# A third room for v, and the first unit of attention handed out ahead of the rest

## The chip, the core and the metric

The kernel runs on one core of a Trainium2 chip. The metric is the device time of one execution in microseconds, the median of several runs. The engines of the core are TensorE (PE, with its weight loads PEld), VectorE (DVE), ScalarE (ACT), GpSimd (POOL) and SyncE (SP), which here issues most of the transfers. Each engine takes its own instructions in order and waits on semaphores for the others.

## What is computed

Linear attention with complex decay over 768 tokens, for 4 batches and 8 heads of 48 elements, and two feed-forward layers (384 to 2048 to 384) behind it on the 3072 tokens:

```python
mag = np.sqrt(a_re * a_re + a_im * a_im)
scale = np.minimum(mag, 0.999) / (mag + 1e-06)
a_re_n, a_im_n = (a_re * scale, a_im * scale)
...
for t in range(S):
    ar, ai = (a_re_n[:, :, t, :, None], a_im_n[:, :, t, :, None])
    new_re = ar * S_re - ai * S_im
    new_im = ar * S_im + ai * S_re
    kv = np.einsum('bhd,bhe->bhde', k[:, :, t], v[:, :, t])
    S_re, S_im = (new_re + kv, new_im)
    y[:, :, t] = np.einsum('bhd,bhde->bhe', q[:, :, t], S_re)
...
h = x @ w_in
g = np.maximum(h, 0.0) + np.log1p(np.exp(-np.abs(h)))
return (g @ w_out).astype(np.float32)
...
h = x @ w_in
g = np.where(h > 0.0, h, alpha * (np.exp(np.minimum(h, 0.0)) - 1.0))
return (g @ w_out).astype(np.float32)
...
x = np.ascontiguousarray(attn_out.transpose(0, 2, 1, 3)).reshape(B * S, H * D)
x = _moe_ref(x=x, **moe_kwargs)
return _moe2_ref(x=x, **moe2_kwargs)
```

The weights arrive as 64-bit floats.

## The kernel before

**Units.** The tokens are cut into 12 units of 256, three to a batch, and each unit into two chunks of 128. For a unit, VectorE forms the cumulative decays (`norm`, `prep`: the lines of it are recorded under L28, as they go through a helper), then in `qk` the decayed queries (`big<-W,qr`) and the decayed keys (`big<-W,tmp`, called KP below). The keys are needed in two forms. Transposed they come from TensorE (`flip`, L296) for the first seven units and from VectorE and memory for the others; with tokens on the partitions they go to memory (`kd`, L271) and come back as `KN` (`load_N`, L327).

**Chunks.** `chunks(u)` then has, for each of the two chunks: scores (L334, two groups of four heads on TensorE), the causal mask on VectorE (P), the outputs from P, v and the state (`outputs`, L358 and L361), and the state's update with KN and v (`update`, L395). Units 0 to 2 and 11 are brought into the layout of the products by TensorE (`relay`, L384); the others go to memory (`xd`) and come back as `xr` (L847). In both cases `split` makes the two parts xh (ScalarE, L404) and xl (VectorE, L405) that the products read.

**v.** `self.V` has two rooms for a chunk's v. `update` of chunk i loads chunk i + 2 into the room that chunk i has just used, so that load waits on TensorE until chunk i's outputs and update are through. SyncE issues it, in line with all its other loads.

**Products.** The first layer goes in steps: eight for a unit, each with two blocks of 128 of the hidden width. `a_s1` is the first product, `a_elem` the softplus (three passes on ScalarE, then L545 and L550 on VectorE), `a_s2` the second product; step n has the first product of n, the elementwise part of n - 1 and the second product of n - 2. All matmuls of the products are recorded at L525. `w_step` decodes one of 32 weight tiles of the layer from 64-bit form, with four instructions on VectorE (L449, L451, L452, L405).

**What sets the order.** One function lets the attention go on between the products. `decays()` is a generator that yields after each piece of a unit's VectorE work, for unit after unit; `stream()` takes a step of it, runs the actions that have fallen due (`DLY` steps after a store the reload, `CH0` steps after the keys' store the start of `chunks(u)`), and then one step of the chunks. `adv(ns)` takes steps until the VectorE work handed out, by a rough count, has reached a due time. Before the first product it is called for `W1` = 24,000 ns, then for `W0` = 2,000 ns at a time with one `w_step` each, up to `G0` = 12, until unit 0's input of the products is there. In the loop over the products it is called twice a step for `STEP` = 2,000 ns. A scheduler of the language then settles the order on each engine, by its own model of when each instruction can run.

Of the kernel before, what the change touches and what calls it, by code (L numbers as in the profile page):

```python
# [38 lines left out]
class Attn:  # L39
    def __init__(self, tc, ctx, flags, bank, net, q, k, v, a_re, a_im):  # L40
        self.tc, self.nc = tc, tc.nc
        self.q, self.k, self.v, self.a_re, self.a_im = q, k, v, a_re, a_im
        P = lambda n, b, **kw: ctx.enter_context(tc.tile_pool(name=n, bufs=b, **kw))
        self.raw = P("raw", 1)
        self.tmp = P("tmp", 3)
        self.wp = P("wp", 1)
        self.bigp = P("bigp", 2)
        self.c1 = P("c1", 1)
        self.ct = P("ct", 1)
        self.kn = P("kn", 2)  # L50
        self.pp = P("pp", 2)
        self.zp = P("zp", 1)
        self.dr = P("dr", 2, space=DRAM)
        self.bank, self.net = bank, net
        self.vec = Paced(self.nc.vector)
        nc = self.nc
        self.mask = self.c1.tile([128, 1, 128], F32, name="mask")
        nc.gpsimd.memset(self.mask, 1.0)
        nc.gpsimd.affine_select(
            out=self.mask, in_=self.mask, pattern=[[0, 1], [1, 128]],  # L60
            compare_op=ALU.is_ge, fill=0.0, base=0, channel_multiplier=-1)
        self.eye = self.c1.tile([128, 128], F32, name="eye")
        nc.gpsimd.memset(self.eye, 1.0)
        nc.gpsimd.affine_select(out=self.eye, in_=self.eye, pattern=[[1, 128]], compare_op=ALU.is_equal,
                                fill=0.0, base=0, channel_multiplier=-1)
        self.T = self.c1.tile([128, 1, 2, 64], F32, name="T")
        nc.gpsimd.memset(self.T[:, :, 0, :], 1.0)
        nc.gpsimd.memset(self.T[:, :, 1, :], 0.0)
        self.X = self.c1.tile([128, 2, 17, 4], F32, name="X")
        self.mh = flags[:, 92:93]  # L70
        nc.gpsimd.memset(self.mh, -0.5)
        self.ph = flags[:, 93:94]
        nc.gpsimd.memset(self.ph, 1.5)
        self.place = self.c1.tile([128, 96], F32, name="place")
        nc.gpsimd.memset(self.place, 0.0)
        for r in range(2):
            o = self.place[64 * r:64 * r + 64, 48 * r:48 * r + 48]
            nc.gpsimd.memset(o, 1.0)
            nc.gpsimd.affine_select(out=o, in_=o, pattern=[[1, 48]], compare_op=ALU.is_equal,
                                    fill=0.0, base=0, channel_multiplier=-1)  # L80
        self.V = []
        for i in range(2):
            t = self.c1.tile([128, 400], F32, name=f"V{i}")
            nc.gpsimd.memset(t[:, 384:400], 0.0)
            self.V.append(t)
        self.s0 = flags[:, 0:12]
        self.fin = flags[:, 12:28].rearrange("p (a b) -> p a b", a=4)
        self.st, self.nx = {}, None
# [21 lines left out]
    def load_v(self, i):  # L110
        b, t0 = i // 6, (i % 6) * 128
        self.nc.sync.dma_start(
            out=self.V[i % 2][:, 0:384].rearrange("t (h d) -> t h d", h=8),
            in_=self.v[b, :, t0:t0 + 128, :].rearrange("h t d -> t h d"))

    def tmpt(self):
# [227 lines left out]
    def outputs(self, u, c):  # L344
        nc = self.nc
        i = 2 * u + c
        QT = self.st["qT", u][:, :, c * 128:(c + 1) * 128]
        V = self.V[i % 2]
        Pt = [self.st.pop(("P", c, g)) for g in range(2)]
        if i % 6 == 0:  # L350
            self.Z = self.bank("Z")[0:96, 0:384].rearrange("p (h e) -> p h e", h=8)
            self.zs = None
        zs = self.zs
        Y = self.bank("sc").rearrange("p (h t) -> p h t", h=4)
        for h in range(8):
            pr, i4 = h % 2, h // 2
            o = Y[64 * pr:64 * pr + 64, i4, :]
            nc.tensor.matmul(out=o, lhsT=V[:, 48 * h:48 * h + 64], rhs=Pt[h // 4][:, h % 4, :],  # L358
                             start=(h < 2), stop=(zs is None and h > 5), skip_group_check=True)
            if zs is not None:  # L360
                nc.tensor.matmul(out=o[0:48], lhsT=zs[:, h, :], rhs=QT[:, h, :],  # L361
                                 start=False, stop=(h > 5), skip_group_check=True)
        self.Y = Y
# [24 lines left out]
    def update(self, u, c):  # L388

        i = 2 * u + c  # L390
        V = self.V[i % 2]
        if i % 6 != 5:
            KN = self.st.pop(("N", u, c))
            for h in range(8):
                self.nc.tensor.matmul(out=self.Z[:, h, :], lhsT=KN[:, h, :], rhs=V[:, 48 * h:48 * h + 48],  # L395
                                      start=(i % 6 == 0 and h == 0), stop=False, skip_group_check=True)
            self.zs = self.zp.tile([96, 8, 48], F32, name="zs", tag="zs")
            self.nc.scalar.activation(out=self.zs, in_=self.Z, func=AF.Copy)
        if i + 2 < 24:
            self.load_v(i + 2)  # L400
# [11 lines left out]

CH0 = 7
DLY = 2
W0 = 2000
W1 = 24000
STEP = 2000
G0 = 12
GA = 4
R0 = 3  # L420
R1 = 2
# [35 lines left out]
END = object()  # L457
# [306 lines left out]
def quick(tc, keep, q, k, v, a_re, a_im, w_in1, w_out1, w_in2, w_out2, out):  # L764
    nc = tc.nc
    with ExitStack() as ctx:
# [32 lines left out]
        def chunks(u):  # L799
# [56 lines left out]
            X[u] = hi, lo  # L856
            yield

        def decays():
            for _ in A.norm(0):  # L860
                yield
            for u in range(NU):
                n = 0
                for _ in A.prep(u):
                    n += 1
                    if n == 2 and u + 2 < NU:
                        A.load_a(u + 2)
                    yield
                yield from A.qk(u)
                if u + 1 < NU:  # L870
                    A.load_qk(u + 1)

        step, acts = 0, []
        ch = {"gen": None}

        def stored(n, u):
            if n != "n":
                acts.append((step + DLY, lambda: A.load_T(u, n)))
                return
            def load():  # L880
                A.load_N(u, 0)
                A.load_N(u, 1)
            acts.append((step + DLY, load))

            def go():
                ch["gen"] = itertools.chain(ch["gen"] or (), chunks(u))
            acts.append((step + CH0, go))

        A.stored = stored
# [1 line left out]
        def stream():  # L891
            nonlocal step, acts
            main = decays()
            busy = True
            while busy or acts or ch["gen"]:
                if busy:
                    busy = next(main, END) is not END
                step += 1
                now_, acts = [f for s, f in acts if s <= step], [x for x in acts if x[0] > step]
                for f in now_:  # L900
                    f()
                r = next(ch["gen"], END) if ch["gen"] else None
                if r is END:
                    ch["gen"] = r = None
                yield r

        st = stream()
# [2 lines left out]
        def adv(ns):  # L910

            nonlocal held, due
            due += ns
            while A.vec.ns < due:
                if held is not None and now < 8 * (held - 1):
                    due = A.vec.ns
                    return
                try:
                    held = next(st)
                except StopIteration:  # L920
                    due = A.vec.ns
                    return
# [5 lines left out]
        A.load_a(1)  # L928
        for net.top in range(LA):
            net.w_load(net.top)  # L930
        adv(W1)
        while 0 not in X:
            adv(W0)
            if net.g < G0:
                net.w_step()
        XR, X2 = {}, {}

        def x_load(b):
# [14 lines left out]
        for n in range(8 * NU + 2):  # L953
            u, p = n // 8, n % 8
            now = n
            if n < 8 * NU:
                while u not in X:
                    adv(1000)
                if n == 8 * NU - 8:
                    for _ in st:  # L960
                        pass
                    actx.close()
                    late = lambda name, bufs, side: ctx.enter_context(
                        tc.tile_pool(name=name, bufs=bufs, side=side, reuse_waits="tile"))
                    net.wp += [late("wts2", 12, "left"), late("wts3", 4, "left")]
                    xps = [late("xb0", 1, "left")]
                    net.w_load(32)
                    net.w_load(33)
                    net.top = 33
                    x_load(0)  # L970
                if n == 8 * NU - 3:
                    x_split(0)
                while net.g < min(32, 4 * n + GA):
                    net.w_step()
                if net.g == 32:
                    net.w_end()
# [86 lines left out]
```

## Time and profile before

| | |
|---|---|
| Median of three runs | 1195.05 us (1192.0 to 1198.69) |
| The profiled execution | 1191.51 us, of it 1189.8 us span |
| TensorE matmul, weight load | 1012.8 us (85%), 946.1 us (80%) |
| VectorE, ScalarE | 810.5 us (68%), 668.5 us (56%) |
| TensorE's mean clock | 0.957 of 2.4 GHz |

How to read it: the first product starts at 115.86 us, the last unit's first product at 742 us. From there TensorE is all but full, with the second layer's weights still decoded up to some 810 us. Between these two times attention and first layer share the engines. A unit's stretch below runs from its first product to that of the next unit; in it TensorE does that unit's products and, in between, attention of the next one. The granted clock of a stretch is a mean of the two levels, 1.2 and 2.4 GHz, in parts of the higher.

### The profile page before, as it was taken

How to read it: one execution, taken by the hardware profiler on the slowest of the kernel's cores; microseconds unless marked ns; L12 is line 12 of the kernel's file. 1: busy time of each engine (PE TensorE's matmuls, PEld its weight loads, DVE VectorE, ACT ScalarE, POOL GpSimd, SP SyncE). 2: the span in 40 equal slices, each digit the busy share in tenths (PEclk: the TensorE clock that was granted, in tenths of full speed). 3: DMA queues.
4: the chain of work that ended last, by engine and by line, in shares of the span. 5: the costliest groups of instructions: out<-in, count | busy, mean ns of one | idle time of the engine just before them, and what ended most of it. 6: DMA issues, size and time to landing. Idle time of an engine off the chain costs nothing.

```text
span 1189.8 us, 18268 instructions
## 1 busy us (share of the span) xinstructions
PE 1012.8 (85%) x7106; PEld 946.1 (80%) x7106; DVE 810.5 (68%) x1521; ACT 668.5 (56%) x1207; POOL 2.2 (0%) x19
## 2 busy tenths in 40 slices
PE   0027889798789989877988999999999999999997
PEld 0016789787689989877888889989999999999996
DVE  4997998596979979786879888894434333343332
ACT  5734866364648566444554568994545444454443
POOL 0000000000000000000000000000000000000000
PEclk9999989798889999887989999999999999999999
DMA  7335451534536263545363665550101000000000
GB/s 231 139 120 145 126 133 43 134 97 83 155 66 179 70 158 115 139 116 137 97 166 107 164 184 174 175 173 1 53 1 53 1 1 27 1 27 1 28 1 29
DMA packets 101823, 114.51 MB, mean 96 GB/s; under 512 B 49760, under 2 KB 78944, under 8 KB 101728
## 3 DMA queue, kind: packets, MB, share of 16 engines
q1 hardware_dynamic: 90272, 105.40, 31.5%
q10 hardware_dynamic: 11456, 7.87, 2.2%
q8 instruction: 57, 0.93, 0.3%
q14 instruction: 38, 0.31, 0.1%
HBM read 77.86 MB, written 35.39 MB: 95 GB/s over the span
## 4 chain that ended last, share of the span: by engine, by line
PE 52%; DMA 22%; DVE 14%; ACT 6%; issue 3%; SPq 1%; ACTq 0%; DVEq 0%
PE b L525 42%; DMA kd<-big 7%; DMA KN<-kd 7%; DVE big L28 4%; DVE tmp L28 4%; PE b L334 3%; PE b L395 3%; DMA wr<-in_moe_w_in_dram 3%; PE b L358 2%; DMA wr<-in_moe_w_out_dram 2%; DMA xr<-xd 2%; ACT w L446 1%; ACT w L445 1%; PE b L361 1%; DMA xd<-ye 1%
## 5 line engine op out<-in xcount | busy, mean ns | idle before, releaser
L525 PE MATMUL b<-xh,w 128*128 128x256 f32 (+1 forms) x1728 | 406.2, 328 | 31.9 <-ACT xh L404 24.2
L525 PEld LDWEIGHTS b<-xh,w 128*128 128x128 f32 x1728 | 295.0, 197 | 55.2 <-ACT xh L404 26.2
L525 PE MATMUL b<-xl,w 128*128 128x256 f32 (+1 forms) x864 | 277.8, 325 | 0.6 <-DVE xl L405 0.6
L525 PE MATMUL b<-gh,w 128*128 128x256 f32 x1152 | 215.0, 288 | 1.7 <-ACT gh L548 1.7
L525 PE MATMUL b<-w,gh 128*128 128x384 f32 x768 | 190.8, 335 | 0.0
L525 PEld LDWEIGHTS b<-gh,w 128*128 128x128 f32 x1152 | 179.0, 195 | 3.9 <-ACT gh L548 2.1
L525 PEld LDWEIGHTS b<-xl,w 128*128 128x128 f32 x864 | 167.5, 196 | 12.9 <-DVE xl L405 1.0
L584 DVE SCALAR_TENSOR_TENSOR t<-t,b 128x512 f32<-128x512 f32 x96 | 65.9, 687 | 149.8 <-ACT t L582 149.8
L525 PE MATMUL b<-gl,w 128*128 128x256 f32 x576 | 158.5, 292 | 3.0 <-DVE gl L550 3.0
L525 PEld LDWEIGHTS b<-w,gh 128*128 128x128 f32 x768 | 140.0, 188 | 7.8
L525 PE MATMUL b<-w,gl 128*128 128x384 f32 x384 | 123.7, 335 | 0.0
L581 ACT ACTIVATE t<-b 128x512 f32<-128x512 f32 x96 | 57.2, 596 | 111.6 <-PE b L525 109.2
L405 DVE TENSOR_TENSOR gl<-t,gh 128x512 fp32r<-128x512 f32 x96 | 66.4, 691 | 71.6 <-ACT gh L404 70.4
L525 PEld LDWEIGHTS b<-gl,w 128*128 128x128 f32 x576 | 108.5, 196 | 4.8 <-DVE gl L550 4.0
L404 ACT ACTIVATE gh<-t 128x512 fp32r<-128x512 f32 x96 | 60.6, 631 | 77.0 <-PE b L525 71.8
L541 ACT ACTIVATE t<-b 128x512 f32<-128x512 f32 x96 | 56.8, 591 | 58.0 <-PE b L525 43.8
L296 PE MATMUL b<-eye,big 128*96 128x128 f32 x112 | 17.0, 294 | 82.3 <-DVE big L28 82.1
L548 ACT ACTIVATE gh<-t 128x512 fp32r<-128x512 f32 x96 | 60.0, 626 | 48.1 <-DVE t L545 24.6
L296 PEld LDWEIGHTS b<-eye,big 128*96 128x96 f32 x112 | 13.2, 135 | 83.3 <-issue 81.6
L28 DVE TENSOR_TENSOR P<-b,mask 128x512 f32<-128x512 f32 x48 | 33.0, 688 | 66.8 <-PE b L334 66.8
L395 PE MATMUL b<-V,KN 128*96 128x48 f32 x320 | 40.5, 288 | 43.2 <-DMA KN<-kd 43.2
L395 PEld LDWEIGHTS b<-V,KN 128*96 128x96 f32 x320 | 38.6, 206 | 46.0 <-issue 38.1
(114 smaller groups left out, 1550.3 us busy)
## 6 DMA issues: line engine op xcount, KB each, us to landing
wr<-in_moe_w_in_dram SPq DMA_DIRECT2D x32, 384.0 KB
wr<-in_moe_w_out_dram SPq DMA_DIRECT2D x32, 384.0 KB
dq<-big SPq DMA_DIRECT2D x12, 768.0 KB
qT<-dq SPq DMA_DIRECT2D x36, 256.0 KB
kd<-big SPq DMA_DIRECT2D x12, 768.0 KB
KN<-kd SPq DMA_DIRECT2D x20, 384.0 KB
ar<-in_a_re_dram SPq DMA_DIRECT2D x12, 384.0 KB
ai<-in_a_im_dram SPq DMA_DIRECT2D x12, 384.0 KB
```

What stands on the lines that cost most here:

```text
L28: return f(*a, **kw)
L296: nc.tensor.transpose(out=ps[0:96, 128 * i:128 * i + 128], in_=W[:, 96 * (4 * g + i):96 * (4 * g + i) + 96], identity=self.eye)
L334: self.nc.tensor.matmul(out=sc[:, h, :], lhsT=KT[:, 4 * g + h, :], rhs=QT[:, 4 * g + h, :], start=(h == 0), stop=(h == 3), skip_group_chec ...
L358: nc.tensor.matmul(out=o, lhsT=V[:, 48 * h:48 * h + 64], rhs=Pt[h // 4][:, h % 4, :], start=(h < 2), stop=(zs is None and h > 5), skip_gro ...
L395: self.nc.tensor.matmul(out=self.Z[:, h, :], lhsT=KN[:, h, :], rhs=V[:, 48 * h:48 * h + 48], start=(i % 6 == 0 and h == 0), stop=False, sk ...
L404: nc.scalar.activation(out=hi, in_=x, func=AF.Copy)
L405: nc.vector.tensor_tensor(out=lo, in0=x, in1=hi.bitcast(F32), op=ALU.subtract)
L525: self.nc.tensor.matmul(out=out, lhsT=lhsT, rhs=rhs, skip_group_check=True, **kw)
L541: nc.scalar.activation(out=t, in_=h, func=AF.Abs)
L548: nc.scalar.activation(out=gh, in_=t, func=AF.Copy)
L581: nc.scalar.activation(out=t, in_=h, func=AF.Relu, scale=-1.0)
L584: nc.vector.scalar_tensor_tensor(out=t, in0=t, scalar=-1.0, in1=h, op0=ALU.add, op1=ALU.max)
```

## The change

`V` gets a third room, and the load of chunk i + 2 goes into the room that chunk i - 1 has used. The scratch for descriptors shrinks from 1024 to 256. Before the first product, `stream()` is stepped one step at a time, with a `w_step` at each step after the sixth, up to 22 of the layer's 32 weights instead of 12. `decays()` sets `alone` when unit 0's keys are done and yields once more; while `alone` is set, the stream does not go on with the next unit's decays, until unit 0's input is there. The same holds while a later unit's input is waited for and chunks are open. If chunks of two units are open, the stream takes two steps of them. `adv` takes at most four steps at a call.

```diff
-        for i in range(2):
+        for i in range(3):
             t = self.c1.tile([128, 400], F32, name=f"V{i}")
...
-            out=self.V[i % 2][:, 0:384].rearrange("t (h d) -> t h d", h=8),
+            out=self.V[i % 3][:, 0:384].rearrange("t (h d) -> t h d", h=8),
...
-W0 = 2000
-W1 = 24000
+S0 = 6
 STEP = 2000
-G0 = 12
+STEPS = 4
+G0 = 22
...
+        def chunked(u):
+            yield from chunks(u)
+            ch["n"] -= 1
+
...
                 yield from A.qk(u)
+                alone["on"] = u == 0
                 if u + 1 < NU:
                     A.load_qk(u + 1)
+                if u == 0:
+                    yield
...
-                ch["gen"] = itertools.chain(ch["gen"] or (), chunks(u))
+                ch["gen"] = itertools.chain(ch["gen"] or (), chunked(u))
+                ch["n"] += 1
...
-                if busy:
+                if busy and not alone["on"]:
                     busy = next(main, END) is not END
...
-                r = next(ch["gen"], END) if ch["gen"] else None
-                if r is END:
-                    ch["gen"] = r = None
+                r = None
+                for _ in range(2 if ch["n"] > 1 else 1):
+                    if ch["gen"] and r is None:
+                        r = next(ch["gen"], END)
+                        if r is END:
+                            ch["gen"] = r = None
                 yield r
...
-            while A.vec.ns < due:
+            for _ in range(STEPS):
+                if A.vec.ns >= due:
+                    break
...
-        adv(W1)
         while 0 not in X:
-            adv(W0)
-            if net.g < G0:
+            next(st)
+            if net.g < G0 and step > S0:
                 net.w_step()
+        alone["on"], due = False, A.vec.ns
...
                 while u not in X:
+                    alone["on"] = bool(ch["gen"])
                     adv(1000)
+                alone["on"] = False
...
-                while net.g < min(32, 4 * n + GA):
+                while net.g < min(32, max(4 * n + GA, G0 + 2 * n)):
                     net.w_step()
...
-    nc = _bacc.Bacc("TRN2", target_bir_lowering=False, num_devices=1, dynamic_dma_scratch_size=1024)
+    nc = _bacc.Bacc("TRN2", target_bir_lowering=False, num_devices=1, dynamic_dma_scratch_size=256)
```

What the scheduler makes of it is seen at three places. The first is VectorE before the first product, where unit 0's first xl is made from the relayed bank; X and T belong to unit 1's decays, f and w to the decoding of weights. Before:

```order
L28 TENSOR_TENSOR tmp<-X 128x256
L28 TENSOR_TENSOR P<-b_582,mask 128x512
L452 SCALAR_TENSOR_TENSOR f<-wr,f 128x384
L28 TENSOR_TENSOR X<-tmp 128x64 x2
L405 TENSOR_TENSOR w<-f,w 128x384
L405 TENSOR_TENSOR xl<-b_630,xh 128x3x128
```

and after:

```order
L28 TENSOR_TENSOR tmp<-X 128x256
L28 TENSOR_TENSOR P<-b_598,mask 128x512
L452 SCALAR_TENSOR_TENSOR f<-wr,f 128x384
L28 TENSOR_TENSOR X<-tmp 128x64 x2
L405 TENSOR_TENSOR w<-f,w 128x384
L405 TENSOR_TENSOR xl<-b_620,xh 128x3x128
```

The same rows stand there, the xl as row 161 of VectorE before and 160 after: nothing has moved at this place.

The second is TensorE at the first update of unit 2, chunk 4 (L395), among unit 1's products; gh and gl are the elementwise results of a step. Before:

```order
L525 MATMUL b3_1755<-gh_2215,w_1430 128x256 x2
L525 MATMUL b3_1755<-gl_2216,w_1430 128x256
L334 MATMUL b4_1601<-qT_1243,kT_1542 128x128 x4
L334 MATMUL b5_1619<-qT_1243,kT_1542 128x128 x4
L395 MATMUL b7_548<-V0_137,KN_1360 96x48 x8
L358 MATMUL b4_1732<-P_1661,V0_137 64x128
```

and after:

```order
L525 MATMUL b2_1584<-gh_1858,w_716 128x256 x2
L525 MATMUL b2_1584<-gl_1859,w_716 128x256
L525 MATMUL b3_1585<-gh_1858,w_716 128x256 x2
L334 MATMUL b4_1885<-qT_1665,kT_1826 128x128 x4
L334 MATMUL b5_1903<-qT_1665,kT_1826 128x128 x4
L525 MATMUL b3_1585<-gl_1859,w_716 128x256
L395 MATMUL b7_581<-V1_139,KN_1726 96x48 x6
L525 MATMUL b2_1584<-gh_1966,w_793 128x256 x2
```

Before, all products of unit 1 stand ahead of the update and none behind it; after, products of unit 1 stand on both sides of it.

The third is TensorE at the first product of unit 5 (from xh), where unit 4's second products end. Before:

```order
L525 MATMUL b3_3616<-gh_4031,w_1283 128x256 x2
L525 MATMUL b3_3616<-gl_4032,w_1283 128x256
L525 MATMUL b1_4070<-xh_4066,w_289 128x256 x2
L525 MATMUL b6_4150<-xh_4066,w_358 128x256 x2
L525 MATMUL b0_4221<-xh_4066,w_471 128x256 x2
L525 MATMUL b2_3615<-gh_4130,w_1410 128x256 x2
L525 MATMUL b3_3616<-gh_4130,w_1410 128x256 x2
```

and after:

```order
L525 MATMUL b3_3505<-gh_4030,w_1054 128x256 x2
L525 MATMUL b3_3505<-gl_4031,w_1054 128x256
L296 MATMUL b4_4100<-eye_122,big_3985 96x128 x4
L296 MATMUL b5_4106<-eye_122,big_3985 96x128 x4
L525 MATMUL b1_3961<-xh_3957,w_201 128x256 x2
L525 MATMUL b6_4040<-xh_3957,w_265 128x256 x2
L525 MATMUL b0_4141<-xh_3957,w_352 128x256 x2
L296 MATMUL b4_4115<-eye_122,big_3985 96x128 x4
```

The transposes of unit 6's keys (L296) stood 63 rows behind unit 5's first product before; now they stand ahead of and among unit 5's first products, and unit 4's last second product is through before them.

## Rows read from the trace of the kernel before

**Rows 1.** The page's part 1: busy us, share of the span, instructions of each engine.

```profile
PE 1012.8 (85%) x7106; PEld 946.1 (80%) x7106; DVE 810.5 (68%) x1521; ACT 668.5 (56%) x1207; POOL 2.2 (0%) x19
```

**Rows 2.** Stretches: length, busy us of PE, PEld, DVE, ACT, POOL, clock, DMA, GB/s.

```profile
115.86:182.17 66.31, 55.96 (x460) 52.05 (x461) 61.60 (x116) 48.84 (x95) 0.00 (x0) 0.92 0.46 129
182.17:244.79 62.62, 53.98 (x444) 51.17 (x444) 46.30 (x109) 30.02 (x50) 0.00 (x0) 0.86 0.31 83
244.79:308.54 63.75, 50.03 (x416) 48.70 (x417) 51.47 (x97) 35.41 (x56) 0.00 (x0) 0.89 0.42 101
308.54:360.50 51.96, 46.69 (x397) 45.17 (x398) 43.44 (x85) 30.44 (x51) 0.00 (x0) 0.90 0.43 110
360.50:410.08 49.58, 47.38 (x436) 46.33 (x435) 45.87 (x87) 35.29 (x56) 0.00 (x0) 1.00 0.44 124
410.08:458.80 48.72, 45.36 (x395) 43.86 (x396) 41.19 (x82) 31.26 (x52) 0.00 (x0) 0.96 0.47 128
458.80:523.30 64.50, 53.69 (x457) 52.24 (x456) 51.82 (x95) 33.12 (x59) 0.00 (x0) 0.90 0.51 135
742.00:1189.80 447.80, 439.95 (x2337) 400.48 (x2335) 196.47 (x326) 238.03 (x437) 0.00 (x0) 1.00 0.12 39
```

**Rows 3.** Waits of TensorE in the whole span: us in total, times, longest.

```profile
PE b L395 <- DMA KN<-kd: 43.2, 11, 7.3
PE b L525 <- ACT xh L404: 24.2, 9, 8.1
```

**Rows 4.** Waits of VectorE, the row on the scores.

```profile
DVE P L28 <- PE b L334: 66.8, 25, 11.5
```

**Rows 5.** Two of VectorE's groups by shape: busy us, mean ns, idle before.

```profile
L28 DVE TENSOR_TENSOR big<-W,tmp 128x1536 f32<-128x1536 f32 x12 | 21.0, 1752 | 0.2
...
L405 DVE TENSOR_TENSOR w<-f,w 128x384 fp32r<-128x384 f32 x64 | 34.9, 552 | 3.0 <-ACT w L404 2.6
```

**Rows 6.** Timeline, unit 2: KP on VectorE, its store and reload on SyncE.

```profile
210.99 1.76 DVE L28 TENSOR_TENSOR big<-W,tmp 128x1536 f32<-128x1536 f32 x1
...
212.77 0.34 SPq L271 DMA_DIRECT2D kd<-big  x1
...
220.59 0.38 SPq L327 DMA_DIRECT2D KN<-kd  x1
```

**Rows 7.** Timeline of TensorE: first update matmuls of units 2 to 9, idle before.

```profile
228.93 1.32 PE L395 MATMUL b<-V,KN 128*96 128x48 f32 x7 [7.29 <-DMA KN<-kd]
...
279.81 1.49 PE L395 MATMUL b<-V,KN 128*96 128x48 f32 x8 [5.61 <-DMA KN<-kd]
...
334.72 0.52 PE L395 MATMUL b<-V,KN 128*96 128x48 f32 x2 [4.74 <-DMA KN<-kd]
...
386.69 1.47 PE L395 MATMUL b<-V,KN 128*96 128x48 f32 x15 [1.36 <-DMA KN<-kd]
...
436.85 1.19 PE L395 MATMUL b<-V,KN 128*96 128x48 f32 x12 [3.36 <-DMA KN<-kd]
...
491.99 1.33 PE L395 MATMUL b<-V,KN 128*96 128x48 f32 x7 [4.49 <-DMA KN<-kd]
...
553.43 1.81 PE L395 MATMUL b<-V,KN 128*96 128x48 f32 x10 [5.79 <-DMA KN<-kd]
...
609.39 1.83 PE L395 MATMUL b<-V,KN 128*96 128x48 f32 x10 [3.61 <-DMA KN<-kd]
```

**Rows 8.** A stretch full of products, columns as in rows 2.

```profile
258.00:264.00 6.00, 6.00 (x53) 6.00 (x52) 6.00 (x8) 4.58 (x8) 0.00 (x0) 1.00 0.72 221
```

**Rows 9.** Timeline of TensorE: first products of units 3 and 10, idle before.

```profile
308.54 1.65 PE L525 MATMUL b<-xh,w 128*128 128x256 f32 x6 [8.11 <-ACT xh L404]
...
695.73 0.97 PE L525 MATMUL b<-xh,w 128*128 128x256 f32 x6 [1.78 <-ACT xh L404]
```

**Rows 10.** Waits of SyncE's queue ahead of the loads of v (L112).

```profile
SPq L112 <- PE b L361: 154.5, 15, 23.1
SPq L112 <- PE b L358: 42.4, 4, 19.1
```

More of the change, by code (lines that the diff above doesn't have):

```diff
@@ L347, in outputs @@
         QT = self.st["qT", u][:, :, c * 128:(c + 1) * 128]
-        V = self.V[i % 2]
+        V = self.V[i % 3]
         Pt = [self.st.pop(("P", c, g)) for g in range(2)]
@@ L390, in update @@
         i = 2 * u + c
-        V = self.V[i % 2]
+        V = self.V[i % 3]
         if i % 6 != 5:
@@ L869, in decays @@
                 yield from A.qk(u)
+                alone["on"] = u == 0
                 if u + 1 < NU:
                     A.load_qk(u + 1)
+                if u == 0:
+                    yield
         step, acts = 0, []
-        ch = {"gen": None}
+        alone = {"on": False}
+        ch = {"gen": None, "n": 0}
         def stored(n, u):
```

## The prediction

> **What bounds the kernel now.** I read first the page's busy shares: no engine is full, TensorE 85% and VectorE 68% [rows 1]. Then the span cut at the first product of each unit of 256 tokens [rows 2]: after 742 us TensorE is busy 439.95 of 447.80 us at full clock. That is the second layer, which the change leaves as it is, so nothing can be won there. Before it, the stretches of 49 to 66 us differ from one another: in the one from 182.17 TensorE is busy 53.98 of 62.62 us and VectorE 46.30, in the one from 360.50 it takes 49.58 us with 47.38 busy. So both engines wait, and not always. TensorE's waits are two [rows 3]: 43.2 us on KN, the keys that go through memory and come back, and 24.2 us on xh, the attention's result made ready for the products. VectorE waits 66.8 us for scores [rows 4], because TensorE takes its instructions in order and the scores of a unit's second chunk stand behind the matmuls that want KN. After long waits the granted clock is lower: 0.86, 0.89 and 0.90 in the three stretches from 182.17 to 360.50, 1.00 in the next [rows 2]. At half clock work takes twice as long, so a stretch loses (1 - clock) times its length: 8.8, 7.0 and 5.2 us there.
>
> **The work itself.** No product, matmul or decode step is added or removed; VectorE, ScalarE and TensorE do the same work. The third room costs one memory fill, on POOL, which has 2.2 us of work in all [rows 1]. The smaller scratch only makes space. So every term is one of order.
>
> **Startup.** The unit handed out alone should leave VectorE earlier. The order says it hardly does: the same pieces of unit 1 still stand between unit 0's on VectorE, and the first xl comes after 160 rows instead of 161. Counting each row with the mean of its shape as in [rows 5], less the 0.08 us by which neighbours overlap, KP of unit 0 (the keys, the last big product of a unit on VectorE) comes 2.7 us of work earlier, but the second xl, which ends the preparation, 1.3 us later. Between them stands the same round trip of KN. I take 0 for the first product; the bounds are 2.7 us either way. In the stretch that follows VectorE is busy 61.60 of 66.31 us [rows 2], so VectorE's order prices it: 61.0 us of work between the second xl of unit 0 and that of unit 1 become 58.5. That is a gain of 2.5; I take **-2**.
>
> **KN.** One round trip worked out, unit 2: KP starts at 210.99 and takes 1.76 us, its store is issued at 212.77, the reload at 220.59 [rows 6], and the first matmul with KN starts at 228.93 after 7.29 us of idle [rows 7]. So 18 us pass from KP to KN, whatever the order. What hides them is the work that stands between on TensorE. In a full stretch 53 matmuls of a product take 6.00 us [rows 8], 0.11 us each. In the order of before, between the product whose elementwise part stands last ahead of KP on VectorE and the matmuls on KN, there are 90 product matmuls, 16 transposes and 8 score matmuls: 10.0 + 4.2 + 2.1 = 16.2 us (a quarter of a microsecond each for the latter). In the new order there are 166 and 16: 22.6 us. KP stands 1.5 us of VectorE work behind that elementwise part before and 0.6 now. Cover rises from 14.8 to 22.0 us, and 7.2 of the 7.29 us go.
> The same count for units 1 to 10, before: 17.2, 14.8, 21.2, 13.0, 20.0, 20.4, 17.3, 14.1, 13.4, 14.9. After: 15.6, 22.0, 30.0, 32.3, 18.6, 11.7, 13.6, 17.0, 13.5, 18.1. Where it rises, the wait of [rows 7] goes, at most by the rise: 7.2 (unit 2), 5.6 (3), 4.7 (4), 2.9 (8), in sum 20.4. Where it falls, a wait grows by the fall: 1.6 (1), 1.4 (5), 8.7 (6), 3.7 (7), in sum 15.4. Net **-5**. Bounds: -20 if the falls are covered, +15 if the rises buy nothing because the wait only goes to the next thing on the same chain.
>
> **xh.** The first product of a unit needs xl. I compare the VectorE work from the last elementwise part of the unit before to xl with the TensorE work between the same two products. Before, units 3 to 11: 1.4, -5.2, -0.8, -5.8, -3.9, -1.3, 0.4, 0.0, -6.2 us of excess; the wait is 8.11 us at unit 3 and 1.78 at unit 10 [rows 9], so an excess of some -4 waits nothing. After: -2.2, -1.8, 2.3, 1.2, -6.4, -2.5, -3.4, 0.0, -8.0. Taking 4 plus the excess, below zero as nothing, the sum goes from 19.8 to 21.6: **+2**. The waits move from units 3, 8 and 9 to 4, 5 and 6, where the new order puts KP and the transposes of the next unit ahead of this unit's first products. Bounds: -8, if the trip of the output through memory alone decides (matmul work behind the last output rises in units 3, 7, 8 and 9), and +5.
>
> **Clock.** In the three stretches from 182.17 to 360.50 the waits on KN of units 2 to 4 and the long one on xh shrink; the 21 us lost to the clock should fall by two thirds, -14. In the two stretches from 360.50 to 458.80, now nearly without loss (0 and 1.9 us), the new waits fall: 10 us on KN and 10 on xh more. I give them the loss that the stretches with such waits have now, 4 and 4 us: +8. Net **-6**, bounds -14 and +4.
>
> **Rooms for v.** SyncE, which issues the loads in order, stands 154.5 and 42.4 us in 19 waits for v's room [rows 10]. No engine waits for v, though, and the load of xr behind it waits for the attention output anyway. Price 0; the other end is the rival on freed loads. In four units the new order puts the load of xr behind those that wait for VectorE's transposes; that is in the xh term, as xl stands late there on VectorE too.
>
> **Sum.** -2 - 5 + 2 - 6 = -11 us on the profiled 1191.51, which lies 3.5 under the median of the runs: 1195.05 - 11 = **1184**. A second count, on VectorE alone: the idle for the scores [rows 4] is cover against chain, and the cover between KP and the second chunk's scores rises by 8.3 us of work in unit 2 (27 instructions become 39), by 1.6 to 2.8 in units 1, 3, 4 and 7, and falls by up to 1.5 in others, 14 us in sum. Some 5 of that I take off for unit 2, where TensorE's own work ahead of those scores grows too. That leaves -9; the two counts agree.
>
> **Rivals.** *Freed loads.* If SyncE's waits for rooms hold back the output's reload, the whole 24.2 us on xh go, with the rest as above but for its +2: 1195 - 13 - 24 = 1158, or 1170 where half of them give way to another wait. For it: the 197 us of waits. Against it: xr is issued right after its data has landed in every unit I looked at. The Trainium skill (Perfetto Trace Analysis, Optimization Strategy) says that gaps that repeat on an engine can mean too few buffers; by that rule the third room is the gain and this case the likely one, while no row here shows an engine that waits for v. With the lower bounds of the other terms, it gets 0.13.
> *Waits change places.* KN and xh net -3, no clock won, startup 0: 1189 to 1200, no change. For it: the attention's chain is as long as before and each unit still needs it. 0.27.
> *The lead costs more than it brings.* The new order has VectorE 12.4 and 17.6 us of work further in the attention when it comes to the first elementwise parts of units 5 and 6. TensorE stands at the transposes of unit 6, ahead of unit 5's first products, until KP of unit 6 is there: 10 us on KN, 10 on xh, 8 of clock, 28 us. It is given back only if unit 6's stretch, now 64.50 us, falls by some 14 (VectorE's part of it falls from 50.9 to 36.7). If half of that fails to come and unit 1's and 2's stretches win 8 instead of 14, the sum is +4 to +8: 1199 to 1203. It decides when the two stretches from 360.50 to 458.80 grow by over 30 us. 0.15.
>
> **How the numbers follow.** The forecast has 0.45, and its own range is 1173 to 1189. Half a per cent, 6 us, is about what a measurement of this kernel can tell from no change. Faster by more: forecast and freed loads, 0.58. Within: 0.27. Slower: 0.15. The range leaves out the far end of the freed loads and of the lead: 1166 to 1201.
>
> **What would show it.** First product at 116 us, within 2. Waits on KN from 43 to some 38, gone in units 2 to 4 and longer at 6 and 7. Stretches: unit 1's and 2's 7 us shorter each, those of units 4 and 5 together some 18 longer, unit 6's 14 shorter, the rest even; the clock near 0.95 in the first and under 0.95 in unit 5's. After the last unit's first product, 447 us as now. It is wrong if the first product comes much earlier, if KN waits stay in units 2 and 3, or if the stretches of units 4 and 5 do not grow.

## The result and the profile after

The changed kernel takes **1164.78 us** (median of 4 runs) beside 1194.19 for the kernel before: a ratio of 0.975, interval 0.9716 to 0.9784, 29 us. The profiled run took 1162.61 us, span 1160.8. The forecast was 1184 and its range began at 1166: the direction was right, the gain was more than twice what was counted.

Part 1 of the page after; [rows 1] is its counterpart.

```profile
PE 1001.1 (86%) x7106; PEld 933.2 (80%) x7106; DVE 810.4 (70%) x1521; ACT 667.2 (57%) x1207; POOL 2.2 (0%) x20
```

With the same 7106 matmuls, TensorE is busy 11.7 us less, and its idle time falls by 17.3 (29.0 of span less 11.7). Not all of the 11.7 can be put down to the clock: 3.3 of them lie ahead of the first product, where the rows show no higher clock after. The first row is the kernel before, the second the changed one, columns as in [rows 2]:

```profile
0.00:115.86 115.86, 25.79 (x157) 21.36 (x157) 90.56 (x205) 61.08 (x132) 2.22 (x19) 1.00 0.53 158
0.00:117.54 117.54, 22.46 (x156) 17.74 (x156) 90.67 (x209) 60.83 (x135) 2.24 (x20) 0.92 0.56 166
```

In units 0 to 10 the busy time falls by 9.0 (547.0 to 538.0), in the second layer it grows by 0.7.

Three waits of TensorE in the kernel before, beside those of [rows 3]:

```profile
PE b L296 <- DVE big L28: 82.1, 2, 81.6
...
PE b L525 <- DVE t L545: 7.4, 8, 2.2
...
PE b L334 <- DMA kT<-dk: 0.6, 1, 0.6
```

Where it waits after the change, and VectorE's row on the scores ([rows 3] and [rows 4]; us, times, longest):

```profile
PE b L296 <- DVE big L28: 86.5, 4, 80.6
PE b L525 <- ACT xh L404: 25.3, 9, 7.6
PE b L395 <- DMA KN<-kd: 15.6, 5, 6.8
PE b L334 <- DMA kT<-dk: 6.3, 2, 6.1
...
DVE P L28 <- PE b L334: 32.3, 13, 7.5
```

KN went from 43.2 to 15.6 and not to 38, xh from 24.2 to 25.3 (+2 was forecast), the scores from 66.8 to 32.3, 34 us where the second count had 9. The waits on KN fall by 27.6 us and all idle time by 17.3 only: kT takes back 5.7, the transposes (L296) 4.4 and xh 1.1. The chain that ended last says the same: the share of transfers on it falls. Its first line before, then after:

```profile
PE 52%; DMA 22%; DVE 14%; ACT 6%; issue 3%; SPq 1%; ACTq 0%; DVEq 0%
```

```profile
PE 58%; DMA 16%; DVE 13%; ACT 8%; issue 4%; SPq 2%; ACTq 0%; DVEq 0%
```

The stretches after, cut as in [rows 2]: units 0 to 10, then the second layer.

```profile
117.54:181.35 63.81, 56.54 (x461) 51.58 (x461) 60.45 (x124) 45.39 (x88) 0.00 (x0) 0.94 0.42 118
181.35:239.04 57.69, 50.85 (x444) 47.68 (x445) 49.81 (x103) 34.01 (x56) 0.00 (x0) 0.97 0.33 90
239.04:291.71 52.67, 46.81 (x416) 45.07 (x416) 48.76 (x91) 34.59 (x56) 0.00 (x0) 1.00 0.46 121
291.71:344.24 52.53, 49.66 (x433) 47.78 (x433) 48.18 (x89) 34.70 (x57) 0.00 (x0) 0.97 0.44 118
344.24:404.74 60.50, 51.64 (x424) 49.06 (x424) 51.09 (x92) 34.50 (x55) 0.00 (x0) 0.89 0.46 129
404.74:461.94 57.20, 48.47 (x408) 47.21 (x408) 49.99 (x90) 34.04 (x56) 0.00 (x0) 0.92 0.49 139
461.94:505.90 43.96, 41.74 (x343) 40.67 (x344) 37.30 (x77) 24.31 (x41) 0.00 (x0) 0.87 0.48 123
505.90:567.45 61.55, 53.14 (x457) 51.78 (x456) 48.58 (x91) 33.14 (x56) 0.00 (x0) 0.94 0.45 122
567.45:613.87 46.42, 46.33 (x400) 44.87 (x401) 42.77 (x86) 27.12 (x47) 0.00 (x0) 0.96 0.51 147
613.87:667.24 53.37, 47.63 (x437) 46.15 (x435) 49.10 (x90) 30.25 (x50) 0.00 (x0) 1.00 0.51 150
667.24:712.64 45.40, 45.23 (x392) 42.12 (x393) 35.97 (x64) 35.28 (x82) 0.00 (x0) 0.96 0.63 195
712.64:1160.80 448.16, 440.64 (x2344) 401.47 (x2342) 197.69 (x327) 239.03 (x438) 0.00 (x0) 1.00 0.12 39
```

Units 7 and 8 of the kernel before, which [rows 2] leaves out:

```profile
523.30:586.06 62.76, 51.93 (x401) 49.80 (x401) 47.66 (x87) 29.91 (x48) 0.00 (x0) 0.86 0.45 111
586.06:643.21 57.15, 48.69 (x400) 46.42 (x400) 48.00 (x90) 29.33 (x51) 0.00 (x0) 0.94 0.52 144
```

After less before: start +1.7; units 0 to 10: -2.5, -4.9, -11.1, +0.6, +10.9, +8.5, -20.5, -1.2, -10.7, +0.9, -0.9; second layer +0.4; in sum -29.0. More than half of it is there at the first product of unit 3 (308.54 before, 291.71 after: -16.8), and -12.2 comes behind it. This cut is used below.

### The profile page after: what moved, and what is told of

Same layout as the page of the kernel before. It is cut to its first block, busy times and chain, and to the rows that moved or that the text cites. A ratio compares the mean times of both kernels' runs of the same rounds, so it can differ in the third digit from the quotient of the medians.

```text
span 1160.8 us, 18255 instructions
## 1 busy us (share of the span) xinstructions
PE 1001.1 (86%) x7106; PEld 933.2 (80%) x7106; DVE 810.4 (70%) x1521; ACT 667.2 (57%) x1207; POOL 2.2 (0%) x20
## 4 chain that ended last, share of the span: by engine, by line
PE 58%; DMA 16%; DVE 13%; ACT 8%; issue 4%; SPq 2%; ACTq 0%; DVEq 0%
PE b L525 49%; DMA kd<-big 4%; DMA KN<-kd 4%; DVE big L28 3%; PE b L334 3%; DVE tmp L28 3%; PE b L395 2%; PE b L358 2%; DMA wr<-in_moe_w_out_dram 1%; ACT w L446 1%; ACT w L445 1%; DMA wr<-in_moe_w_in_dram 1%; PE b L361 1%; DVE W L28 1%; DMA kT<-dk 1%
## 5 line engine op out<-in xcount | busy, mean ns | idle before, releaser
L525 PE MATMUL b<-xh,w 128*128 128x256 f32 (+1 forms) x1728 | 405.6, 328 | 32.3 <-ACT xh L404 25.3
L525 PE MATMUL b<-gl,w 128*128 128x256 f32 x576 | 156.0, 286 | 1.4 <-DVE gl L550 1.4
L405 DVE TENSOR_TENSOR gl<-t,gh 128x512 fp32r<-128x512 f32 x96 | 66.4, 692 | 72.0 <-ACT gh L404 70.9
L296 PE MATMUL b<-eye,big 128*96 128x128 f32 x112 | 19.3, 320 | 86.8 <-DVE big L28 86.5
L548 ACT ACTIVATE gh<-t 128x512 fp32r<-128x512 f32 x96 | 60.0, 627 | 55.5 <-PE b L525 37.2
L296 PEld LDWEIGHTS b<-eye,big 128*96 128x96 f32 x112 | 14.8, 147 | 88.5 <-issue 85.5
L525 PEld LDWEIGHTS b<-w,gl 128*128 128x128 f32 x384 | 71.7, 188 | 0.1
L550 DVE TENSOR_TENSOR gl<-t,gh 128x512 fp32r<-128x512 f32 x96 | 65.4, 685 | 8.1 <-ACT gh L548 7.0
L545 DVE SCALAR_TENSOR_TENSOR t<-b,t 128x512 f32<-128x512 f32 x96 | 65.5, 683 | 5.6 <-ACT t L543 5.4
```

The costliest lines, as they stand in the source:

```text
L296: nc.tensor.transpose(out=ps[0:96, 128 * i:128 * i + 128], in_=W[:, 96 * (4 * g + i):96 * (4 * g + i) + 96], identity=self.eye)
L405: nc.vector.tensor_tensor(out=lo, in0=x, in1=hi.bitcast(F32), op=ALU.subtract)
L525: self.nc.tensor.matmul(out=out, lhsT=lhsT, rhs=rhs, skip_group_check=True, **kw)
L545: nc.vector.scalar_tensor_tensor(out=t, in0=h, scalar=0.0, in1=t, op0=ALU.max, op1=ALU.add)
L548: nc.scalar.activation(out=gh, in_=t, func=AF.Copy)
L550: nc.vector.tensor_tensor(out=gl, in0=t, in1=gh.bitcast(F32), op=ALU.subtract)
```

## The experiments

**One part undone, one part alone.** Two rooms for v in the changed kernel leave TensorE's and VectorE's orders as they are.

```diff
-        for i in range(3):
+        for i in range(2):
...
-        V = self.V[i % 3]
+        V = self.V[i % 2]
```

> The changed kernel with two rooms for v, as before; the order of the instructions on TensorE and VectorE is the same as in the changed kernel, row for row but for buffer names. Theory of the order (the gain comes from what stands between what on TensorE and VectorE): 1163 to 1168 us, as the changed kernel, and SyncE's waits for v grow from 201 us back towards 219 without an engine waiting for v. Rival of the rooms (the gain comes from loads that no longer stand behind the wait for v's room): 1180 to 1194 us, and TensorE's waits on KN or xh grow by 10 us or more.

> The changed kernel with two rooms for v; TensorE's and VectorE's orders are the same as in the changed kernel. Room theory: 5 to 8 us above the changed kernel of this call, 1170, with the waits for KN 5 us longer (20 against 15), in the stretches of units 5 and 7. Rival (the room does nothing): within 3 us of it.

> The changed kernel once more, beside three others on one chip. If the third room is worth what the first comparison showed (1164.8 here, 1170.9 with two rooms), it comes in at 0.975 of the kernel before and 6 us below the version with two rooms beside it; if that difference was one of chips, the two agree within 3 us.

Measured: 1170.87 (0.9828, 0.9781 to 0.9875) and, on another chip, 1168.75 (0.9798, 0.9757 to 0.984) beside 1163.29 (0.975, 0.9699 to 0.98) of the changed kernel. Both lie between the two ranges of the first expectation: most of the gain needs no third room, but not all of it. Side by side on one chip the room is worth 5.5 us, and none of the four runs with two rooms is as fast as the slowest with three; across chips it is 6.1 us by the times and 9 by the ratios. I take some 6. The intervals of the ratios overlap at their ends. Next, the new start in the kernel before (the change's lines on S0, G0, the start's loop and `alone` for unit 0; two rooms, single steps, no hold-back later):

> The kernel before with the new start alone (unit 0 alone, decode at each step up to 22 weights); two rooms, no holding back for later units, no double steps of the chunks. By the count of cover ahead of KN, units 2, 4 and 6 gain 6.4, 3.7 and 1.8 us, units 3, 7, 8 and 10 lose 3.1, 1.6, 1.2 and 6.1. Theory of the order, with falls counted in full: KN waits as before, 1186 to 1194 us. The same with falls that are covered elsewhere: KN waits down by 10 us or more, 1176 to 1185 us. Rival of the rooms: 1190 to 1196 us.

Measured: 1193.5, 1.0018 (0.9987 to 1.0049). Then the changed kernel without one of its two hold-backs:

```diff
-                alone["on"] = u == 0
+                alone["on"] = False
```

> The changed kernel without the one line that lets unit 0 go alone. The order falls back to near that of before (72% of TensorE's and 79% of VectorE's rows of the first layer match before, 47% match the changed kernel) although 22 weights are still handed out early, there are three rooms and the chunks go ahead. Theory of the order: 1188 to 1196 us, KN waits over 35 us. Rival of the rooms: 1165 to 1175 us. Rival of the weights (22 decoded early make the gain): 1165 to 1175 us.

```diff
-                    alone["on"] = bool(ch["gen"])
```

> The changed kernel without the line that holds the next unit's decays back while a later unit's input is waited for. The order is that of the new start alone, not of the changed kernel, from unit 2 on. Theory of the order: as the new start alone, within 3 us of it, and slower than the changed kernel by 8 to 25 us, with KN waits at units 3 and 4 that the changed kernel does not have. Rival of the rooms: 1163 to 1170 us, as the changed kernel.

Measured: 1191.78 (0.9991, 0.9964 to 1.0019) and 1192.71 (1.0013, 0.9977 to 1.0049). And the later hold-back alone in the kernel before; and the changed kernel with single steps (`range(1)` for `range(2 if ch["n"] > 1 else 1)`):

> The kernel before with the hold-back alone (chunks ahead of the next products), with the old start, two rooms, single steps. The start alone made no difference and the changed kernel without the hold-back none either. If the two only win together, this is within 4 us of the kernel before, 1187 to 1195. If the hold-back with single steps wins by itself, it is at 1165 to 1180.

> The changed kernel without the double steps where two units' chunks are at hand; its order differs from row 2455 of TensorE on, about from unit 7. If the gain is made by the start and the hold-back in units 1 to 6 (and by unit 6's stretch, which follows from them), this stays within 4 us of the changed kernel, 1161 to 1169. If the double steps make the gain of units 6 to 8 (some 30 us of it), it comes to 1175 to 1190.

Measured: 1201.44 (1.0069, 1.0035 to 1.0102), outside both theories: the later hold-back alone loses; and 1160.35 (0.9746, 0.9686 to 0.9806), so the double steps are worth nothing that shows. **In these runs the two hold-backs win only together.** The cap of four steps in `adv`, which the two single edits leave out, was not run apart. The steps of `stream()`, counted while the program is built, show how the two meet: before, 44 steps of the preparation are out at the first product, after 23. With the new start alone the product loop, waiting for unit 1, draws 19 more, and from unit 1's first product on the count is that of before to within one. With the later hold-back alone there is a lead of preparation, so the loop waits only at units 3, 5, 7 and 9, and the preparation is held for 30 steps in all. With both, it is held for 81: 15, 12, 14, 12, 12, 8, 0 and 8 steps at units 1 to 8. That these counts make the time is not shown.

In the three kernels that gain nothing, the waits on KN are down too, to 34 to 37 us. But without the later hold-back TensorE's busy time is up by 13 us, and its waits on an elementwise part of the products (t, L545) go from 7.4 to 15.4. Part 1 of that kernel's page, and its row on t:

```profile
PE 1026.0 (86%) x7106; PEld 955.9 (80%) x7106; DVE 812.1 (68%) x1521; ACT 668.3 (56%) x1207; POOL 2.2 (0%) x20
...
PE b L525 <- DVE t L545: 15.4, 13, 2.6
```

**The round trip itself.** The keys are reloaded from the store of the unit before, so that nothing waits for this unit's store.

```diff
-        kd = self.st["kd", u][:, c * 128:(c + 1) * 128, :]...
+        kd = self.st["kd", max(u - 1, 0)][:, c * 128:(c + 1) * 128, :]...
```

> The kernel before, with the keys KN of a unit read from the stored keys of the unit before it (the right keys are left out of the state's update; all loads, stores and matmuls stay). The reload no longer waits for this unit's store. The schedule moves some instructions for it. Theory 1 (the round trip of KN is what TensorE pays for, and the clock falls after it): the 43 us of waits on KN go to under 5 and the time comes down to 1145 to 1170, as far as the change or further. Rival (another wait takes its place, xh or the scores' kT on the same chain): KN waits gone, but the waits on xh and kT grow by 15 or more, and the time is 1180 to 1195.

> The same edit in the changed kernel. Theory 1: only the 15 us on KN that are left can go, 1145 to 1160, so that the difference between the two kernels with old keys is 10 us or less where it is 30 with the right ones. Rival: the changed kernel gains as little as the kernel before, and the 30 us between them stay.

Measured: 1177.18 (0.9863, 0.9779 to 0.9947) and 1160.31 (0.9714, 0.9641 to 0.9787). Neither theory hit the first, which lies between the two: 38 us of waits on KN go, 19 us of time (16 by the ratio). TensorE's waits in the kernel before with old keys:

```profile
PE b L334 <- DMA kT<-dk: 20.7, 5, 7.9
PE b L525 <- ACT xh L404: 16.5, 6, 5.9
...
PE b L395 <- DMA KN<-kd: 5.6, 1, 5.6
```

The second reload, kT, takes half of it over (0.6 before). The changed kernel had little left to gain there, 3 to 4 us; the two stay 17 us apart, where theory 1 had 10 or less and its rival 30.

**What stands in the trip.** Between the store of the keys and their reload SyncE issues ar and ai in units 0 to 8. A trip is here the time from the issue of that store to the first matmul with KN. (The trips of 14.9 to 21.4 us that are named below are those of units 2 to 8; units 0 and 1 took 14.0 and 11.5.) Without these loads from unit 2 on:

```diff
     def load_a(self, u):
+        if u >= 2:
+            self.st["a", u] = self.akeep[u % 2]
+            return
```

> The kernel before without the loads of ar and ai from unit 2 on (units use the data of units 0 and 1; the work on them stays). In the trace these two loads of 384 KB stand between the store of the keys and their reload in units 0 to 8, where the trip from the store's issue to the first matmul takes 14.9 to 21.4 us; in units 9 to 11, without them, 11.5 to 14.5. Collision theory: the trips of units 2 to 8 fall to 11 to 15, the waits on KN from 43 to 20 to 28, the time by 10 to 25. Rival (the trip has its length from the store and the reload themselves): trips within 1.5 us of the old ones, time within 6 us.

> The same edit in the changed kernel, where KN waits are 15 us and the two loads stand in the trip in units 0 to 7 only. Collision theory: 4 to 10 us faster, KN waits under 10. Rival: within 3 us.

Measured: 1162.11 (0.9744, 0.9673 to 0.9814) and 1136.26 (0.9506, 0.9436 to 0.9576): 34 us (31 by the ratio), and 29 by the ratios in the changed kernel, more than the collision theory had. The work left out is traffic only, so this is a price, not a version. The same loads moved, with nothing left out (from unit 3 on; in the third run they go behind the first KN of a unit, in the other two behind the last):

```diff
+            if behind is not None:
+                nc.gpsimd.tensor_copy(out=t[0:1, 0:1], in_=behind[0:1, 0, 0:1])
             nc.sync.dma_start(out=t, in_=s[b, :, t0:t0 + 256, :]...
...
-                    if n == 2 and u + 2 < NU:
-                        A.load_a(u + 2)
+                    if n == 2 and u == 0:
+                        A.load_a(2)
...
                 A.load_N(u, 1)
+                if u + 3 < NU:
+                    A.load_a(u + 3, A.st.get(("N", u, 1), A.st["N", u, 0]))
```

> The kernel before with the two loads of a (ar, ai, 384 KB each) issued behind the reload of the keys: an element of KN is copied on POOL into the first element of each room, so that the load waits until KN has landed; nothing is left out. Collision theory (the loads lengthen the trip of KN when they stand in it): trips of units 2 to 8 of 11 to 15 us, KN waits 43 to under 25, 1165 to 1182. Rival (the traffic costs as much wherever it stands): the waits move to kT, xh or to the store of the next keys, 1185 to 1200.

> The same edit in the changed kernel, behind the second KN. Collision theory: 1140 to 1156, KN waits under 8. Rival: 1158 to 1170, the change's own time.

> The changed kernel with the loads of a behind the first KN, which leaves its order nearer to that of the changed kernel (360 rows of difference on VectorE against 1160). Collision theory: 1142 to 1158. Rival: 1158 to 1170.

Measured: 1166.83 (0.9765, 0.9736 to 0.9794), 1152.76 (0.965, 0.9619 to 0.9681) and **1148.11** (0.9606, 0.9576 to 0.9637). All three lie in the ranges of the collision theory, and the last beats both kernels. The moved loads give back some 27 of the 34 us and some 16 of the 29; what the rest is was not looked into, and the schedule moves some instructions for the edit. The trip of unit 8 shows it: issues on SyncE (start, length) and the first matmul with KN, in the kernel before, then with the loads behind:

```profile
532.01 0.38 SPq L271 DMA_DIRECT2D kd<-big  x1
535.01 0.34 SPq L309 DMA_DIRECT2D dk<-big  x1
535.84 0.62 SPq L96 DMA_DIRECT2D ar<-in_a_re_dram  x1
536.66 0.60 SPq L96 DMA_DIRECT2D ai<-in_a_im_dram  x1
541.71 0.37 SPq L327 DMA_DIRECT2D KN<-kd  x1
...
553.43 1.33 PE L395 MATMUL b<-V,KN 128*96 128x48 f32 x7 [5.79 <-DMA KN<-kd]
```

```profile
518.58 0.42 SPq L273 DMA_DIRECT2D kd<-big  x1
521.58 0.34 SPq L311 DMA_DIRECT2D dk<-big  x1
528.38 0.37 SPq L329 DMA_DIRECT2D KN<-kd  x1
...
532.05 1.30 PE L397 MATMUL b<-V,KN 128*96 128x48 f32 x9 [1.95 <-DMA KN<-kd]
```

The store takes as long as before (9.7 and 9.8 us to the reload's issue); it is the reload, up to the first matmul, that falls from 11.7 to 3.7 us. In units 2 to 8 it took 6.6 to 11.7 before and takes 3.5 to 4.7 with the loads behind. The Trainium skill (DMA: Bandwidth & Descriptors, Rules for kernel authors) advises to issue a transfer early and to wait for it late; here loads issued as early as their room allowed cost 27 us in the kernel before and some 16 in the changed one, because they stood ahead of a reload that was waited for. The same section says that transfers issued from different engines all run on the same 16 DMA engines and interleave; no run here shows how they interleave, as SyncE issues all of these, and the trips show only that the reload takes 11.7 us with the two loads ahead of it and 3.7 without.

All kernels at the cut (first product of unit 3; from there to the end of the span), against the kernel before:

| kernel | to unit 3 | behind it | waits on KN |
|---|---|---|---|
| before | 308.54 | 881.3 | 43.2 |
| changed; again; single steps | -16.8; -15.1; -16.6 | -12.2; -14.8; -15.3 | 15.6; 14.7; 18.4 |
| changed, two rooms; again | -13.9; -15.1 | -7.0; -8.6 | 20.4; 17.6 |
| new start alone | -3.5 | +10.0 | 37.2 |
| without unit 0's hold-back | -3.9 | +2.3 | 34.2 |
| without the later hold-back | -7.5 | +13.6 | 34.5 |
| later hold-back alone | +8.8 | +5.2 | 45.9 |

And the changed kernel against the kernel before where both have the same edit:

| edit in both | to unit 3 | behind it | KN, before and changed |
|---|---|---|---|
| none | -16.8 | -12.2 | 43.2, 15.6 |
| old keys | -17.4 | -0.6 | 5.6, 5.2 |
| no loads of a | -21.8 | +1.9 | 9.6, 4.4 |
| loads of a behind the first KN (changed), behind the last (before) | -19.1 | -1.7 | 12.0, 2.7 |
| loads of a behind the last KN in both | -17.0 | +3.0 | 12.0, 5.2 |

These are single profiles, and the edits shift the order by themselves; but the four pairs with an edit say one thing. The gain up to unit 3 stays (3 to 4 us of it are the start's with old keys and with the loads behind); the 12 us behind it are there only while TensorE waits long for KN. With old keys neither kernel waits for KN behind the first product, and the gain up to unit 3 is still 17.4.

## Why the prediction was right and wrong

- **Up to unit 3: right in the numbers.** Forecast 0 for the first product, -2 for unit 0, -14 for units 1 and 2, in sum -16; measured +1.7, -2.5 and -16.0, in sum -16.8. The start came at 117.54, within the 2 us given. The waits on KN of units 1 to 3 fell by 10.1 where 11.2 were counted. But the pair with old keys keeps its gain there without any wait on KN, so that KN's cover makes it is not shown. The lead's price agrees in the sum too, +18 forecast for units 4 and 5 and +19.4 measured, but in part by luck, as the three parts it was made of add up to 28: the waits on xh in these stretches grew by 9.1 (10 counted) and the busy time by 7.4 (8 for the clock), while KN, counted at +10, fell by 2.1, and the transposes of unit 6 waited 4.8 for VectorE instead. In the whole span xh is +1.1 (+2 forecast).
- **The term that failed is KN from unit 3 on.** By the count the waits of units 3 to 10 change by -5.6, -4.7, +1.4, +8.7, +3.7, -2.9, 0, 0: +0.6. They changed by -5.6, -4.7, +0.1, -2.3, -2.3, -5.8, -3.6, -1.0: -25.1. (Units 0 to 2 gave 2.5 where 5.6 were counted: 3.95 us are left in unit 2, and the wait of unit 0, which was not counted, grew by 2.0.) In the whole span -27.6 stands where -5 was forecast, beyond the bound of -20; 10.3 us of it came back in TensorE's other waits. Two steps of the term were wrong.
- **First step: a fall of cover was made a wait of its own.** Only work was counted as cover. In units 6 and 7, where cover falls by 8.7 and 3.7, TensorE stands on something else during the same trip: +12.4 us were counted, -4.5 came. The changed kernel, idle before each in brackets; the keys are stored at 400.95 and at 453.30:

```profile
400.57 1.92 PE L296 MATMUL b<-eye,big 128*96 128x128 f32 x8 [4.82 <-DVE big L28]
...
404.74 1.65 PE L525 MATMUL b<-xh,w 128*128 128x256 f32 x6 [2.25 <-ACT xh L404]
...
417.29 0.88 PE L395 MATMUL b<-V,KN 128*96 128x48 f32 x8 [1.11 <-DMA KN<-kd]
...
461.94 1.65 PE L525 MATMUL b<-xh,w 128*128 128x256 f32 x6 [7.62 <-ACT xh L404]
...
472.63 1.68 PE L395 MATMUL b<-V,KN 128*96 128x48 f32 x12 [2.21 <-DMA KN<-kd]
```

  The waits on xh, 2.25 and 7.62 us, lie inside the trips, and products at a clock of 0.92 and 0.87 take longer: both hide KN. I had summed KN, xh and clock as if they followed one another. The bound "-20 if the falls are covered" named this; the value was taken too near the other end.
- **Second step: "18 us pass from KP to KN, whatever the order".** From the store's issue to the first matmul it is 11.5 to 21.4 us before. In unit 8 the new order issues the reload ahead of ar and ai, and the trip falls from 21.4 to 12.4. In unit 9 it falls from 14.5 to 11.4; neither load stands in that trip in either kernel, and why it falls was not looked into. Unit 8 after, issues on SyncE and the first matmul, which has no idle ahead of it:

```profile
506.94 0.46 SPq L271 DMA_DIRECT2D kd<-big  x1
511.06 0.34 SPq L309 DMA_DIRECT2D dk<-big  x1
515.30 0.37 SPq L327 DMA_DIRECT2D KN<-kd  x1
515.77 0.62 SPq L96 DMA_DIRECT2D ar<-in_a_re_dram  x1
...
519.33 0.63 PE L395 MATMUL b<-V,KN 128*96 128x48 f32 x6
```

  The waits of 5.79 and 3.61 us went with it, where 2.9 and 0 were counted. Unit 8's stretch, forecast even, lost 10.7; unit 6's lost 20.5 where 14 were forecast.
- **Clock: mis-sized.** -6 was forecast; the busy time of units 0 to 10 fell by 9.0. By (1 - clock) times length, as in the prediction, units 1 to 3 went from 21.0 to 3.3 us (-14 forecast) and units 4 and 5 from 1.9 to 11.2 (+8 forecast), so the clock moved where it was said to. Left out were the other six stretches, 10 us in sum, half of it in unit 7 (0.86 before, 0.94 after). By this price all eleven give 19 us, twice the 9.0 by which the busy time fell: it counts TensorE as busy all the time at the lower level, and its work there as twice as long. In [rows 9] six product matmuls take 1.65 us at a granted clock of 0.50 and 0.97 at 1.00, which is 1.7 times. That -6 came near to -9.0 is in part luck, too high a price on too few stretches.
- **Rooms for v: not 0 but some 6 us, and behind unit 3** (-7.0 and -8.6 against -12.2 to -15.3). The rival on freed loads was right that the room counts, but not by its path, the output's reload: xh is 24.9 and 23.8 us with two rooms and 25.3 and 24.8 with three, while KN is 20.4 and 17.6 with two and 15.6 and 14.7 with three. [rows 10] leave out a third row, 22.0 us in 3 waits on L395. With it SyncE's waits for v's room are 218.9 us before and 222.8 after (not the 201 of the expectation for two rooms), and 239.6 and 237.9 with two rooms. The Trainium skill (Perfetto Trace Analysis, Optimization Strategy) says that a gap which repeats on the engine that should be saturated can mean too few buffers; by that rule the third room would be the gain, and most of it, some 23 of 29 us, came without. How the room shortens the transfers was not isolated; the reload of unit 6 is issued 12.7 and 11.5 us after the store with two rooms, 10.7 and 9.8 with three.
- **The second count** had the same flaw: on VectorE, too, the waits for the scores follow KN, 34 us down and not 9. Its agreement was no proof, since both counts used one idea of cover.
- The rivals of waits that change places and of a lead that costs more fell: units 4 and 5 grew by 19.4, under the 30 that the second needed. What moves the clock within a stretch stays open, and so does by which wait the gain up to unit 3 comes, and why it needs both hold-backs beyond the count of steps above.

## What to carry to other kernels

Before a trip through memory is taken as a constant, list what its queue issues between store and reload: here two loads that nobody needed yet doubled the reload, and moving them gave the kernel before nearly as much as the whole change (27 us beside 29). Waits of one engine that fall into the same trip hide one another; as units 6 and 7 show here, they are not to be added up. Where two edits act on the same lead, try them together before either is dropped.

## What was not expected of the hardware

From its issue to the first matmul, a reload of 384 KB took 3.5 to 4.7 us without, and 6.6 to 11.7 with, two loads of the same size issued 3 to 9 us ahead of it (units 2 to 8). Leaving those loads out is worth 29 to 34 us in a kernel whose transfer engines are busy 31 to 64% in the stretches of units 0 to 10: here the mean share did not show such a trip.
